# Attention's opening, four mask transfers a head, and an order planned with other costs

## The chip, the core and the metric

The kernel runs on one core of a Trainium2 chip. The metric is the time of one execution in microseconds on the device. An execution before the change took 792.61 us (median of three, 789.0 to 793.27). Engines are named as in the profile: PE is TensorE, PEld its weight load, DVE VectorE, ACT ScalarE, POOL GpSimd, SP SyncE, whose queue issues nearly all transfers. A q behind a name (SPq) is the engine's own sequencer.

## The reference

Attention over 16 heads (2 batches of 8), 768 positions and 64 dimensions, in which a query sees only the keys of its own bucket, and then two MoE-like layers on the result:

```python
q_bits = (np.einsum('bhsd,dk->bhsk', q, proj) > 0)      # 6 bits; k_bits likewise
mask = q_bucket[:, :, :, None] == k_bucket[:, :, None, :]
scores = np.where(mask, scale * q @ k.T, -1e9)
attn = np.exp(scores - max); attn = attn / (np.sum(attn) + 1e-09)
out = attn @ v                                         # x: 1536 tokens x 512
x = (h * tanh(softplus(h))) @ w_out,  h = x @ w_in     # first layer, w_in 512x2048
x = elu(h) @ w_out,  h = x @ w_in                      # second layer
```

## The kernel before, in words

All is float32. A product in full precision is made of three products of a high and a low part (`fp32r`); so nearly every operand exists twice, as a cast (high) and a subtraction (low).

**A head.** `prepare(g)` reads the head's k and q (`rw`, 64 rows each), splits them into `z` (high L343, low L345) and moves the halves by four transfers inside SBUF (L350 to L354) into the operand `qkt`, a tile of four slots. The bits of the buckets come from nine small matmuls (`project`, tile `pj`) of z against the random projection `sp`; a threshold (L368) turns the sums into masks (`bits`: 1 or -2^60), and six transfers (`mask`, L373) carry them into rows 64 to 75 of two slots of `qkt`. `V` is read and split for two heads at a time (L381 to L388).

**A tile** is 128 queries against 768 keys (`tile_ops`, six a head, 96 in all, numbered 0 to 95). Its scores `st` are eight matmuls: four over slots of 128 rows (the products of high and low parts) and four over 76 rows (the other products and the mask rows, which add 0 for equal buckets and a huge negative number otherwise). VectorE takes the row maximum (`pt`, `mx`, `nb`), ScalarE the exponential with the sum (`sm`). Two tiles at a time then go through `value_ops`: transposes on TensorE (`tu`), high part by ScalarE (`pth`), low part by VectorE (`ptl`), products with V (`xt`). ScalarE copies `xt` out (`xr`).

**A pair of heads.** When the second head of a pair is done, transfers on SP (`xs`, `xr`, L498 to L504) bring the halves together, GpSimd adds them (L506), TensorE transposes the reciprocals of the sums (`r`, L484), VectorE multiplies (L513), and x is split into `x_hi` and `x_lo`. `xt`, `pj` and `r` share a ring of two PSUM buffers.

**What sets the order.** Operations are recorded with a cost for each engine that may do them, a latency, a priority and the buffers they use; `Plan.run` simulates the engines with these numbers and emits the instructions in the planned order, engine by engine. On the chip each engine then does its list strictly in this order, and waits where an operand or buffer isn't ready. Priorities of the steps come from the tables `OFF` and `ODD`, in units of a tile; `CH` says which engines may do a step. A transfer on SP costs 450 in the plan (ns), and lands after a latency of 2300 to 6000. The MoE phase (`moe`) is planned the same way after it.

Of the kernel before, what the change touches and what calls it, by code (L numbers as in the profile page):

```python
# [10 lines left out]
F32R = mybir.dt.float32r  # L11
# [24 lines left out]
WARM = 10  # L36
NEARLY = 3
# [4 lines left out]
OFF = {'rh': -12.0, 'cp': -4.75, 'ld': -12.75, 'sp': -2.0, 'pj': 1.5, 'bits': -14.75, 'mk': -5.5, 'v': -13.5, 'S': 0.0, 'max': -0.25, 'exp': 12.0, 'sum': -5.25, 'T': 0.25, 'hi': 7.5, 'lo': -5.25, 'R': 7.0, 'pv': 2.0, 'xc': -6.25, 'xa': -34.25, 'xn': 3.25, 'xh': -6.5, 'xm': 9.25}  # L42
ODD = {'lo': [-0.5, 2.0, -1.5, -1.0, -4.5, 0.0], 'T': [-4.5, 1.0, 0.5, 0.0, 0.0, 1.0], 'pv': [3.0, 1.5, 0.0, -0.5, -0.5, -0.5], 'exp': [2.5, 1.5, 0.5, 1.0, 2.0, 0.0], 'hi': [1.0, -2.0, -2.5, 0.0, 3.0, 1.0], 'S': [1.0, 0.0, 1.0, 0.0, 0.5, 0.0], 'xc': [1.0, 0.0, 0.0, 1.0, 2.0, 0.0], 'max': [1.0, 0.5, 0.5, 0.5, 3.0, 2.0]}
# [142 lines left out]
def kernel(ctx, tc, qk, v, w, tab, out):  # L186
# [13 lines left out]
    NB = 6  # L200
# [85 lines left out]
    def attention(p, ap, pss, pst, psx, h_r):  # L286
        ident = ap.tile([128, 128], F32, name="ident")
        cst = ap.tile([128, 2 + NR], F32, name="cst")
        sp = ap.tile([128, 2, 384], F32R, name="sp")
        least, value = cst[:, 0:1], cst[:, 1:2]  # L290

        def tables(e):


            nc.vector.tensor_scalar(out=cst[:, 2 + NB:2 + 3 * NB], in0=cst[:, 2 + NB:2 + 3 * NB], scalar1=-1.0, scalar2=None,
                                    op0=ALU.mult)
            pr = cst[:, 2:2 + NR].unsqueeze(1).to_broadcast([128, 3, NR])
            hi, lo = (sp[:, j].rearrange("p (c n) -> p c n", c=3)[:, :, 0:NR] for j in range(2))
            nc.vector.tensor_copy(out=hi, in_=pr)
            nc.vector.tensor_tensor(out=lo, in0=pr, in1=f32(hi), op=ALU.subtract)  # L300
# [9 lines left out]
        bits_r = ring(2, [128, TH], F32R, "bits")  # L310
# [22 lines left out]
        def prepare(g):  # L333

            pr = NQ * g

            def at(name):
                return pr + OFF[name] if g else -50

            wt, rw, z = Buf(w_r, f"qkt{g}"), Buf(rw_r, f"rw{g}"), Buf(z_r, f"z{g}")  # L340
            ld = p.op({SP: 450}, lambda e: nc.sync.dma_start(out=rw.tile, in_=qk[g]), (), [rw], at('ld'), lat=4000)
# [24 lines left out]
            o = p.op({PE: 1080}, project, [lo, first[0]], [z, pj], at('pj'))  # L366
            bits = Buf(bits_r, f"bits{g}")
            o = p.op({DVE: dve(TH) + 110}, lambda e: nc.vector.tensor_scalar(  # L368
                out=bits.tile, in0=pj.tile[:, 0:TH], scalar1=least, scalar2=value, op0=ALU.is_ge, op1=ALU.mult),
                [o], [pj, bits], at('bits'))  # L370

            def mask(r, slot, c):
                return lambda e: nc.sync.dma_start(out=f32(wt.tile[64:64 + 2 * NB, slot, c * TH:(c + 1) * TH]),  # L373
                                                   in_=f32(bits.tile[32 * c + r:32 * c + r + 2 * NB]))
# [3 lines left out]
            kv[g] = wt, deps  # L378
            if g % 2 == 0:
                vr, vt = Buf(vr_r, f"vr{g}"), Buf(vt_r, f"vt{g}")  # L380
                ld = p.op({SP: 450}, lambda e: nc.sync.dma_start(out=vr.tile, in_=v[g // 2]), [deps[3]], [vr], pr - 4, lat=6000)  # L381

                def v4():
                    return vr.tile.rearrange("p k (j d) -> p k j d", j=2)
                h = p.op(pick('v', {ACT: act(S, False), DVE: 500, POOL: 1100}),
                         lambda e: copy(e, vt.tile[:, :, :, 0:64], v4()), [ld], [vr, vt], pr + OFF['v'])
                lo = p.op({POOL: pool(S)}, lambda e: sub(
                    e, vt.tile[:, :, :, 64:128], v4(), f32(vt.tile[:, :, :, 0:64])), [h], [vr, vt], pr + OFF['v'])  # L388
                V[g // 2] = (vr, vt, ld, lo)

        def tile_ops(i):

            g, t = steps[i]
            wt, wdeps = kv[g]
# [22 lines left out]
            o = p.op({ACT: act(S, False) + 140}, lambda e: nc.scalar.activation(  # L417
# [5 lines left out]
            if t == NQ - 1 or late and t % 2:  # L423
                r = slice(t - 1 if late else 0, t + 1)
                s = p.op(pick('eps', {DVE: 70, POOL: 250}), lambda e: eng(e).tensor_scalar(
                    out=sm.tile[:, r], in0=sm.tile[:, r], scalar1=1e-9, scalar2=None, op0=ALU.add),
                    sums[r], [sm], order(i, 'sum'))
                s = p.op({DVE: 76}, lambda e: nc.vector.reciprocal(out=rc.tile[:, r], in_=sm.tile[:, r]),
                         [s], [sm, rc], order(i, 'sum'))
                n = r.stop - r.start  # L430
                s = p.op({POOL: 150 + 80 * n}, lambda e: nc.gpsimd.tensor_copy(
                    out=rb.tile[:, r, g % 2], in_=rc.tile[:, r].unsqueeze(2).to_broadcast([128, n, 64])),
                    [s], [rc, rb], order(i, 'sum'))
                for j in range(r.start, r.stop):
                    ready.setdefault(j, []).append(s)
# [7 lines left out]
        def value_ops(i):  # L443
# [44 lines left out]
            if g < BH - 2:  # L488
# [26 lines left out]
                h = p.op(pick('xh', {ACT: act(S, False), DVE: 500, POOL: 1100}), lambda e: copy(e, x_hi[:, kt, to], xe.tile),  # L515
# [22 lines left out]
        def setup():  # L538
            nc.vector.memset(f32(sp), 0.0)
            make_identity(nc, ident)  # L540
            first[0] = p.op({ACT: 700}, lambda e: nc.scalar.dma_start(out=cst, in_=tab), (), (), -1e4, 2700)
            p.op({ACT: 1300}, lambda e: nc.scalar.preload_act_table_set("exp_and_others"), [first[0]], (), -1e3)
# [13 lines left out]
        first = [None]  # L556
# [215 lines left out]
```

## Time and profile before

| | |
|---|---|
| runs | 789.0, 792.61, 793.27 us |
| the profiled execution | 792.94 us, span from first to last instruction 791.2 us |
| mean granted clock of TensorE | 0.986 of full |
| PE busy | 763.6 us (97%) |
| DVE, ACT, POOL busy | 594.5, 418.3, 290.5 us |

Attention fills the span up to about 260 us, the MoE layers the rest. The shares of the whole span mix the two, so the rows below are taken by stretch. "Granted clock" is the share of full speed that the chip allowed TensorE.

### The profile page before, as it was taken

The numbers are of one execution on the slowest core, as the hardware profiler recorded it, in microseconds if no ns is written. First come the engines' busy times: TensorE is split into PE (matmuls) and PEld (weight loads), VectorE is DVE, ScalarE is ACT, GpSimd is POOL, SyncE is SP. The second block draws the span as 40 slices with busy tenths as digits, with TensorE's granted clock in tenths as the row PEclk, the third lists the DMA queues.
The fourth block names the chain that finished last, engine by engine and source line by source line (L and its number), as shares of the span: only waits on it lengthen the run. The fifth ranks groups of instructions, "written<-read, shape, count | busy, mean of one in ns | idle before, by whom it ended". The sixth has DMA issues, their size and how long they took to land.

```text
span 791.2 us, 11274 instructions
## 1 busy us (share of the span) xinstructions
PE 763.6 (97%) x4042; PEld 662.8 (84%) x4042; DVE 594.5 (75%) x1084; ACT 418.3 (53%) x800; POOL 290.5 (37%) x248
## 2 busy tenths in 40 slices
PE   4999999999988999999999999999999999999998
PEld 3998998998987888888888888888888888888886
DVE  2787798888779875456756776699977789989852
ACT  0686787877777654443433333447555434444420
POOL 3345355345133242323223332783323342233320
PEclk8899999999999999999999999999999999999999
DMA  6485555555431132111221122111221112121112
GB/s 173 135 217 138 151 154 147 143 142 132 115 97 51 54 107 80 54 54 55 80 80 54 53 66 78 44 54 55 88 97 55 53 54 81 54 80 54 54 66 94
DMA packets 24728, 71.07 MB, mean 90 GB/s; under 512 B 4256, under 2 KB 5408, under 8 KB 24672
## 3 DMA queue, kind: packets, MB, share of 16 engines
q1 hardware_dynamic: 24528, 70.34, 29.8%
q8 instruction: 32, 0.52, 0.3%
q14 instruction: 24, 0.20, 0.1%
q10 hardware_dynamic: 144, 0.01, 0.0%
HBM read 43.00 MB, written 3.15 MB: 58 GB/s over the span
## 4 chain that ended last, share of the span: by engine, by line
PE 83%; DVE 6%; DMA 4%; ACT 3%; SPq 2%; POOL 1%; issue 1%; DVEq 0%; ACTq 0%; POOLq 0%
PE h L580 66%; PE xt L472 5%; PE st L409 5%; PE tu L459 5%; DVE ptl L235 3%; DVE pt L412 2%; PE pj L363 2%; ACT pt L417 2%; DMA xr<-xr 2%; DMA wraw<-in_w_dram 1%; SPq L373 1%; ACT pth L464 1%; POOL xr L506 1%; SPq L349 1%; DVE xr L513 0%
## 5 line engine op out<-in xcount | busy, mean ns | idle before, releaser
L235 POOL TENSOR_TENSOR wt<-wt,whi 128x512 f32<-128x512 f32 x64 | 84.0, 1313 | 318.0 <-ACT whi L230 312.6
L580 PE MATMUL h<-x_hi,whi 128*128 128x512 f32 x384 | 149.7, 390 | 0.0
L580 PE MATMUL h<-glo,whi 128*128 128x512 f32 x384 | 149.4, 389 | 0.0
L580 PE MATMUL h<-x_hi,wlo 128*128 128x512 f32 x384 | 149.4, 389 | 0.0
L580 PE MATMUL h<-x_lo,whi 128*128 128x512 f32 x384 | 149.4, 389 | 0.0
L580 PE MATMUL h<-ghi,whi 128*128 128x512 f32 x384 | 149.4, 389 | 0.0
L580 PE MATMUL h<-ghi,wlo 128*128 128x512 f32 x384 | 149.4, 389 | 0.0
L417 ACT ACTIVATE pt<-pt,nb 128x768 f32<-128x768 f32 x96 | 90.2, 940 | 43.8 <-DVE nb L415 42.7
L235 DVE TENSOR_TENSOR ptl<-tu,pth 128x512 fp32r<-128x512 f32 x144 | 96.3, 687 | 16.8 <-ACT pth L464 16.4
L264 ACT ACTIVATE ws<-wraw 128x512 f32<-128x512 f32 x64 | 43.4, 678 | 117.0 <-POOL wlo L282 112.4
L409 PE MATMUL st<-qkt 76*128 76x384 f32 (+1 forms) x384 | 88.2, 359 | 10.8 <-DMA qkt<-bits 6.3
L412 DVE TENSOR_SCALAR_CACHE_REDUCE pt<-st 128x768 f32<-128x768 f32 x96 | 90.0, 949 | 9.0 <-PE st L409 8.9
L464 ACT CAST pth<-tu 128x512 fp32r<-128x512 f32 x144 | 82.4, 586 | 21.9 <-PE tu L459 20.1
L282 POOL TENSOR_TENSOR wlo<-wt,ws 128x512 fp32r<-128x512 f32 x64 | 86.1, 1346 | 6.7 <-DVE ws L277 2.0
L235 DVE TENSOR_TENSOR glo<-h,ghi 128x512 fp32r<-128x512 f32 x96 | 65.4, 687 | 28.8 <-ACT ghi L230 28.4
L459 PE MATMUL tu<-ident,pt 128*128 128x128 f32 x576 | 84.5, 278 | 2.2 <-DVE ptl L235 1.5
L580 PEld LDWEIGHTS h<-ghi,whi 128*128 128x128 f32 x384 | 72.1, 188 | 15.1
L580 PEld LDWEIGHTS h<-glo,whi 128*128 128x128 f32 x384 | 72.1, 188 | 15.0 <-DVE glo L235 0.2
L580 PEld LDWEIGHTS h<-x_hi,wlo 128*128 128x128 f32 x384 | 72.1, 188 | 15.0
L580 PEld LDWEIGHTS h<-ghi,wlo 128*128 128x128 f32 x384 | 72.1, 188 | 14.9
L680 DVE TENSOR_TENSOR y_acc<-h,y_acc 128x512 f32<-128x512 f32 x72 | 48.3, 687 | 48.2 <-PE h L580 48.1
L580 PEld LDWEIGHTS h<-x_hi,whi 128*128 128x128 f32 x384 | 72.1, 188 | 14.8
(64 smaller groups left out, 1250.3 us busy)
## 6 DMA issues: line engine op xcount, KB each, us to landing
wraw<-in_w_dram SPq DMA_DIRECT2D x64, 512.0 KB
qkt<-z SPq DMA_DIRECT2D x32, 384.0 KB
rw<-in_qk_dram SPq DMA_DIRECT2D x16, 384.0 KB
qkt<-z SPq DMA_DIRECT2D x32, 192.0 KB
vr<-in_v_dram SPq DMA_DIRECT2D x8, 384.0 KB
out_dram<-y_acc SPq DMA_DIRECT2D x12, 256.0 KB
xs<-xr SPq DMA_DIRECT2D x14, 192.0 KB
qkt<-bits SPq DMA_DIRECT2D x96, 12.0 KB
```

What stands on the lines that cost most here:

```text
L235: eng(e).tensor_tensor(out=out, in0=a, in1=b, op=ALU.subtract)
L264: o1 = p.op({ACT: act(n, False)}, lambda e: nc.scalar.activation(out=s.tile, in_=high().bitcast(F32), func=AF.Square), [ld], [raw, s], prio)
L282: o9 = p.op({POOL: pool(n)}, lambda e: nc.gpsimd.tensor_tensor(out=flat(lo), in0=t.tile, in1=s.tile, op=ALU.add), [o6, o8], [t, s, lo], prio)
L363: nc.tensor.matmul(pj.tile[:, 0:TH], lhsT=sp[:, b, c * 96:c * 96 + 128], rhs=z.tile[:, a, c * TH:(c + 1) * TH], start=(n == 0), stop=(n == 8))
L409: nc.tensor.matmul(st.tile[:, c, 0:HS], lhsT=wt.tile[0:n, q, t * 128:(t + 1) * 128], rhs=wt.tile[0:n, 2 + q, c * HS:(c + 1) * HS], start=( ...
L412: o = max_op = p.op({DVE: dve(S)}, lambda e: nc.vector.tensor_scalar(out=half(pt.tile), in0=st.tile[:, :, 0:HS], scalar1=-MASKED / SCALE, ...
L417: o = p.op({ACT: act(S, False) + 140}, lambda e: nc.scalar.activation(out=pt.tile, in_=pt.tile, func=AF.Exp, bias=nb.tile, scale=SCALE, ac ...
L459: nc.tensor.transpose(tu.tile[:, k, j], pt.tile[:, (2 * b + k) * 128:(2 * b + k + 1) * 128], ident)
L464: o = p.op({ACT: act(512)}, lambda e, tu=tu, ks=ks: nc.scalar.copy(out=hi.tile[:, ks], in_=flat(tu)), [o], [tu, hi], order(i, 'hi'))
L472: nc.tensor.matmul(xt.tile[:, 0:TH], lhsT=vt.tile[:, k, g % 2], rhs=m.tile[:, k], start=(k == 0 and j == 0), stop=(k == NKT - 1 and j == 1))
L580: nc.tensor.matmul(t.tile, lhsT=a.tile[:, k], rhs=r, start=(k == 0 and j == 0), stop=(k == 3 and j == 2))
L680: y = p.op({DVE: dve(n)}, lambda e, ya=ya, t=t: nc.vector.tensor_tensor(out=ya, in0=t.tile, in1=ya, op=ALU.add), [x, Y[m, c]], [t], prio)
```

## The change

- Head 0's masks are no longer transferred: four VectorE instructions (`direct`) write them into the operand, 12 rows x 384 columns each. Two of head 0's four operand copies may be issued from ScalarE's queue.
- For the other heads the projection works on two halves of 384 columns (six matmuls for nine), the threshold is 384 wide, and four mask transfers take the place of six.
- The tables for the projection are made before z is split, not after.
- Head 1's z is cast by ScalarE. The addition of 1e-9 moves from GpSimd to VectorE (`CH['eps']`).
- After head 1's projection, TensorE multiplies zeros 16 times (`hold`).
- The planner's numbers change: SP costs 400 to 760 for 450, latencies of 2200 to 4600 for 2300 to 4300, a dearer exponential, cheaper GpSimd casts; `OFF` and `ODD` are replaced.

```diff
-OFF = {'rh': -12.0, 'cp': -4.75, 'ld': -12.75, ...
+OFF = {'rh': 27.75, 'cp': -6.25, 'ld': 29.75, ...
-CH = {'rh': ('POOL',), 'v': ('POOL',), 'xh': ('ACT', 'POOL'), 'eps': ('POOL',)}
+CH = {'rh': ('POOL',), 'v': ('POOL',), 'xh': ('ACT', 'POOL'), 'eps': ('DVE',)}
...
-            h = p.op({DVE: 500} if g == 0 else pick('rh', {DVE: 500, ACT: act(S, False), POOL: 1100}),
+            h = p.op({DVE: 500} if g == 0 else {ACT: act(S, False)} if g == 1 else pick('rh', {..., POOL: 830}),
...
-                return lambda e: nc.sync.dma_start(out=f32(out()), in_=f32(in_()))
+                return lambda e: (nc.scalar if e == ACT else nc.sync).dma_start(out=f32(out()), in_=f32(in_()))
+            two = {SP: 650, ACT: 400} if g == 0 else {SP: 650}
-            if g == 0:
-                first[0] = p.op({DVE: 450}, tables, [first[0], lo], (), -50)
...
                 for a, b in ((0, 0), (0, 1), (1, 0)):
-                    for c in range(3):
-                        nc.tensor.matmul(pj.tile[:, 0:TH], lhsT=sp[:, b, c * 96:c * 96 + 128],
-                                         rhs=z.tile[:, a, c * TH:(c + 1) * TH], start=(n == 0), stop=(n == 8))
+                    for c in range(2):
+                        nc.tensor.matmul(pj.tile[:, 0:HS], lhsT=sp[:, b, 64 * (1 - c):64 * (1 - c) + 128],
+                                         rhs=z.tile[:, a, c * HS:(c + 1) * HS], start=(n == 0), stop=(n == 5))
...
-            for c in range(3):
-                for r, slot in ((0, 1), (2 * NB, 3)):
-                    deps.append(p.op({SP: 450}, mask(r, slot, c), [o], [bits, wt], at('mk'), lat=2300))
+            if g == 0:
+                def direct(e, c, s):
+                    r = slice(64 * c + 32 * s, 64 * c + 32 * s + 2 * NB)
+                    nc.vector.tensor_scalar(out=wt.tile[64:64 + 2 * NB, 1 + 2 * s, c * HS:(c + 1) * HS], in0=pj.tile[r, 0:HS],
+                                            scalar1=cst[r, 0:1], scalar2=cst[r, 1:2], op0=ALU.is_ge, op1=ALU.mult)
+                for c, k in ((0, 1), (1, 1), (0, 0), (1, 0)):
+                    deps.append(p.op({DVE: dve(HS)}, lambda e, c=c, k=k: direct(e, c, k), [o], [pj, wt], at('bits')))
+            else:
...
+                for c in range(2):
+                    for k in range(2):
+                        deps.append(p.op({SP: 760}, mask(c, k), [o], [bits, wt], at('mk'), lat=2700))
...
-                    XS[g // 2] = xs, p.op({SP: 450}, ..., parts, [xr, xs], order(i, 'xm'), lat=2300)
+                    XS[g // 2] = xs, p.op({SP: 650}, ..., parts, [xr, xs], order(i, 'xm'), lat=3000)
...
+            if i == 0:
+                hold = Buf(tu_r, "hold")
+                p.op({PE: 175 * HOLD}, lambda e: spin(HOLD, hold), [kv[1][2]], [hold], -40)
```

What it does to the order, at three places. First SP's list from the start, before (`rw` is a head's read, `qkt<-z` the operand copies, `qkt<-bits` the masks, `vr` V; the number is the head):

```order
L341 DMA rw1_103<-in_qk_dram 128x768
L349 DMA qkt0_111<-z0_106 64x2x768
L349 DMA qkt0_111<-z0_106 64x768
L349 DMA qkt0_111<-z0_106 64x1536
L349 DMA qkt0_111<-z0_106 64x768
L341 DMA rw2_130<-in_qk_dram 128x768
L349 DMA qkt1_132<-z1_108 64x2x768
L349 DMA qkt1_132<-z1_108 64x768
L349 DMA qkt1_132<-z1_108 64x1536
L373 DMA qkt0_111<-bits0_135 12x256 x6
L381 DMA vr0_158<-in_v_dram 128x768
L373 DMA qkt1_132<-bits1_150 12x256 x6
```

and after:

```order
L342 DMA rw1_103<-in_qk_dram 128x768
L350 DMA qkt0_114<-z0_109 64x2x768
L350 DMA qkt1_118<-z1_111 64x2x768
L350 DMA qkt0_114<-z0_109 64x768
L350 DMA qkt1_118<-z1_111 64x768
L350 DMA qkt1_118<-z1_111 64x1536
L350 DMA qkt1_118<-z1_111 64x768
L342 DMA rw2_160<-in_qk_dram 128x768
L342 DMA rw3_164<-in_qk_dram 128x768
L382 DMA qkt1_118<-bits1_162 12x384 x3
L390 DMA vr0_174<-in_v_dram 128x768
L382 DMA qkt1_118<-bits1_162 12x384
```

Head 0's masks and two of its copies (now in ScalarE's list) are gone from SP; V stands behind one more read and three masks of head 1.

TensorE's list from the start, before (`st` with the tile's number, `pj` with the head's):

```order
L553 MATMUL warm_89<-x_lo_65 128x384 x10
L363 MATMUL pj0_120<-z0_106,sp_82 128x256 x9
L363 MATMUL pj1_137<-z1_108,sp_82 128x256 x9
L409 MATMUL st0_166<-qkt0_111 128x384 x4
L409 MATMUL st1_172<-qkt0_111 128x384 x4
L363 MATMUL pj2_183<-z2_156,sp_82 128x256 x9
L409 MATMUL st2_198<-qkt0_111 128x384 x4
```

and after:

```order
L563 MATMUL warm_89<-x_lo_65 128x384 x10
L363 MATMUL pj0_120<-z0_109,sp_82 128x384 x6
L363 MATMUL pj1_131<-z1_111,sp_82 128x384 x6
L563 MATMUL hold_143<-x_lo_65 128x384 x16
L418 MATMUL st0_169<-qkt0_114 128x384 x4
L418 MATMUL st1_176<-qkt0_114 128x384 x4
L418 MATMUL st2_190<-qkt0_114 128x384 x4
```

The zero products stand between the second projection and the first scores, and the third projection has gone behind eight score tiles.

SP's list where heads 4 and 5 are done and head 8 is prepared, before:

```order
L349 DMA qkt8_1551<-z8_1197 64x1536
L349 DMA qkt8_1551<-z8_1197 64x768
L373 DMA qkt8_1551<-bits8_1571 12x256 x6
L502 DMA xs4_1408<-xr5_1489 64x768
L504 DMA xr4_1254<-xr5_1489 64x768
L381 DMA vr8_1654<-in_v_dram 128x768
```

and after:

```order
L350 DMA qkt8_1550<-z8_1240 64x1536
L350 DMA qkt8_1550<-z8_1240 64x768
L511 DMA xs4_1379<-xr5_1426 64x768
L513 DMA xr4_1193<-xr5_1426 64x768
L390 DMA vr8_1667<-in_v_dram 128x768
L382 DMA qkt8_1550<-bits8_1686 12x384 x4
```

The two transfers of x have moved from behind the masks to ahead of them, and V too.

## Rows read from the trace of the kernel before

**Rows 1.** Windows, attention proper and MoE: stretch, length, busy us, clock, DMA.

```profile
30.00:236.00 206.00, 195.76 (x1464) 190.03 (x1463) 170.72 (x417) 160.48 (x341) 85.89 (x83) 0.98 0.56 144
260.00:787.00 527.00, 527.00 (x2348) 436.70 (x2346) 388.10 (x590) 233.36 (x412) 185.35 (x139) 1.00 0.19 67
```

**Rows 2.** Timeline of PE, five of the projections: start, length, in brackets idle before.

```profile
38.58 1.24 PE L363 MATMUL pj<-z,sp 128*128 128x256 f32 x9
...
143.97 1.23 PE L363 MATMUL pj<-z,sp 128*128 128x256 f32 x9
...
159.89 1.34 PE L363 MATMUL pj<-z,sp 128*128 128x256 f32 x9 [1.42 <-DVE xr L513]
...
173.68 1.24 PE L363 MATMUL pj<-z,sp 128*128 128x256 f32 x9
...
235.35 1.23 PE L363 MATMUL pj<-z,sp 128*128 128x256 f32 x9
```

**Rows 3.** Groups by line, 30 to 236 us: busy us, mean ns, idle before.

```profile
L417 ACT ACTIVATE pt<-pt,nb 128x768 f32<-128x768 f32 x85 | 79.9, 940 | 19.2 <-DVE nb L415 18.1
L412 DVE TENSOR_SCALAR_CACHE_REDUCE pt<-st 128x768 f32<-128x768 f32 x83 | 77.6, 949 | 0.0
...
L368 DVE TENSOR_SCALAR bits<-pj,cst 128x256 fp32r<-128x256 f32 x12 | 6.5, 539 | 0.7 <-PE pj L363 0.2
L513 DVE TENSOR_TENSOR xr<-r,xr 128x384 f32<-128x384 f32 x12 | 6.3, 552 | 14.0 <-POOL xr L506 13.4 <-PE r L484 0.6
L484 PE MATMUL r<-ident,rb 128*128 128x128 f32 x36 | 6.2, 284 | 0.0
...
L428 DVE RECIPROCAL rc<-sm 128x6 f32<-128x6 f32 (+1 forms) x15 | 2.7, 180 | 1.6 <-POOL sm L425 1.6
```

**Rows 4.** The chain that ended last, 143 to 163 us: start, us, what.

```profile
143.43 0.71 PE st L409 x4
...
148.64 0.26 ACT xr L230
...
153.81 3.44 DMA xr<-xr
...
157.42 1.84 POOL xr L506
```

**Rows 5.** Timeline of SP's queue, at the opening and at that boundary.

```profile
13.14 5.58 SPq L373 DMA_DIRECT2D qkt<-bits  x6
...
147.51 5.64 SPq L373 DMA_DIRECT2D qkt<-bits  x6
153.25 0.52 SPq L502 DMA_DIRECT2D xs<-xr  x1
```

**Rows 6.** Timeline of PE, 0 to 31 us.

```profile
8.55 3.57 PE L363 MATMUL pj<-z,sp 128*128 128x256 f32 x15 [1.12 <-DVE sp L300]
12.33 0.59 PE L409 MATMUL st<-qkt 128*128 128x384 f32 x2 [0.22 <-DMA qkt<-z]
18.49 0.66 PE L409 MATMUL st<-qkt 76*128 76x384 f32 x1 [5.57 <-DMA qkt<-bits]
...
29.90 0.36 PE L472 MATMUL xt<-pth,vt 128*128 128x256 f32 x1
```

**Rows 7.** Windows in the opening, columns as in rows 1 (PE, PEld, DVE, ACT, POOL).

```profile
5.00:15.00 10.00, 5.05 (x21) 3.99 (x20) 4.51 (x6) 0.00 (x0) 4.37 (x4) 0.83 0.91 226
12.00:15.00 3.00, 0.71 (x3) 0.30 (x2) 0.55 (x1) 0.00 (x0) 1.26 (x2) 1.00 1.09 292
20.00:25.00 5.00, 5.00 (x19) 5.00 (x20) 2.60 (x7) 1.54 (x3) 2.66 (x2) 0.50 0.28 89
```

**Rows 8.** Timeline of DVE, 0 to 12 us.

```profile
4.84 0.96 DVE L235 TENSOR_TENSOR z<-rw,z 128x768 fp32r<-128x768 f32 x1
```

**Rows 9.** Timeline of POOL, 0 to 35 us.

```profile
21.88 0.82 POOL L232 CAST vt<-vr 128x768 fp32r<-128x768 f32 x1 [5.51 <-DMA vr<-in_v_dram]
22.78 1.84 POOL L235 TENSOR_TENSOR vt<-vr,vt 128x768 fp32r<-128x768 f32 x1
```

More of the change, by code (lines that the diff above doesn't have):

```diff
@@ L36 @@
 WARM = 10
+HOLD = 16
 NEARLY = 3
@@ L296, in tables @@
                                     op0=ALU.mult)
-            pr = cst[:, 2:2 + NR].unsqueeze(1).to_broadcast([128, 3, NR])
-            hi, lo = (sp[:, j].rearrange("p (c n) -> p c n", c=3)[:, :, 0:NR] for j in range(2))
+            pr = cst[:, 2:2 + NR].rearrange("p (s n) -> p s n", s=2)
+            hi, lo = (sp[:, j, 64:128].rearrange("p (s n) -> p s n", s=2)[:, :, 0:2 * NB] for j in range(2))
             nc.vector.tensor_copy(out=hi, in_=pr)
@@ L340, in prepare @@
             wt, rw, z = Buf(w_r, f"qkt{g}"), Buf(rw_r, f"rw{g}"), Buf(z_r, f"z{g}")
-            ld = p.op({SP: 450}, lambda e: nc.sync.dma_start(out=rw.tile, in_=qk[g]), (), [rw], at('ld'), lat=4000)
-            h = p.op({DVE: 500} if g == 0 else pick('rh', {DVE: 500, ACT: act(S, False), POOL: 1100}),
+            ld = p.op({SP: 400}, lambda e: nc.sync.dma_start(out=rw.tile, in_=qk[g]), (), [rw], at('ld'), lat=4000)
+            h = p.op({DVE: 500} if g == 0 else {ACT: act(S, False)} if g == 1 else pick('rh', {DVE: 500, ACT: act(S, False), POOL: 830}),
                      lambda e: copy(e, z.tile[:, 0], rw.tile), [ld], [rw, z], at('rh'))
@@ L365, in project @@
                         n += 1
[L366 to L374, printed above, removed]
@@ L375, in prepare, with mask @@
-            for c in range(3):
-                for r, slot in ((0, 1), (2 * NB, 3)):
-                    deps.append(p.op({SP: 450}, mask(r, slot, c), [o], [bits, wt], at('mk'), lat=2300))
-            kv[g] = wt, deps
+            o = pj_op = p.op({PE: 1050}, project, [lo, first[0]], [z, pj], at('pj'))
+            if g == 0:
[6 more added lines that the diff above has]
+            else:
+                bits = Buf(bits_r, f"bits{g}")
+                o = p.op({DVE: dve(HS)}, lambda e: nc.vector.tensor_scalar(
+                    out=bits.tile, in0=pj.tile[:, 0:HS], scalar1=least, scalar2=value, op0=ALU.is_ge, op1=ALU.mult),
+                    [o], [pj, bits], at('bits'))
+                def mask(c, s):
+                    r = slice(64 * c + 32 * s, 64 * c + 32 * s + 2 * NB)
+                    return lambda e: nc.sync.dma_start(out=f32(wt.tile[64:64 + 2 * NB, 1 + 2 * s, c * HS:(c + 1) * HS]),
+                                                       in_=f32(bits.tile[r]))
+                for c in range(2):
+                    for k in range(2):
+                        deps.append(p.op({SP: 760}, mask(c, k), [o], [bits, wt], at('mk'), lat=2700))
@@ L540, in setup @@
             make_identity(nc, ident)
-            first[0] = p.op({ACT: 700}, lambda e: nc.scalar.dma_start(out=cst, in_=tab), (), (), -1e4, 2700)
-            p.op({ACT: 1300}, lambda e: nc.scalar.preload_act_table_set("exp_and_others"), [first[0]], (), -1e3)
+            ld = p.op({ACT: 700}, lambda e: nc.scalar.dma_start(out=cst, in_=tab), (), (), -1e4, 2200)
+            p.op({ACT: 1300}, lambda e: nc.scalar.preload_act_table_set("exp_and_others"), [ld], (), -1e3)
+            first.append(p.op({DVE: 450}, tables, [ld], (), -1e3))
             warm = Buf(tu_r, "warm")
@@ L554, in spin @@
                                  start=True, stop=True)
-        first = [None]
+        first = []
         last, gates = [], []
@@ L744 @@
         tab[(D if r < 2 else 0):(2 * D if r < 2 else D), 2 + r * NB:2 + (r + 1) * NB] = proj
-    for c in range(3):
-        tab[32 * c:32 * c + NB, 0] = tab[32 * c + 3 * NB:32 * c + 4 * NB, 0] = TINY
-        tab[32 * c:32 * c + 2 * NB, 1] = 1.0
-        tab[32 * c + 2 * NB:32 * c + 4 * NB, 1] = -BIG
+    for c in (0, 64):
+        tab[c:c + NB, 0] = tab[c + 32 + NB:c + 32 + 2 * NB, 0] = TINY
+        tab[c:c + 2 * NB, 1] = 1.0
+        tab[c + 32:c + 32 + 2 * NB, 1] = -BIG
     units = []
```

43 lines of the change are left out of this document (22 added, 21 removed).

## The prediction

> **What bounds the kernel now.** I read the busy time by stretch first [rows 1]. From 260 us to 787 us, in the two MoE layers, TensorE is busy for 527.00 of 527.00 us at full clock. Nothing in that code changes, so I take this stretch as it is: whatever the change does, it moves the moment at which attention hands over. In attention proper (30 to 236 us) TensorE is busy 195.76 of 206 us, VectorE 170.72 and ScalarE 160.48. TensorE is the nearest to a bound, but the waits have to be read one by one.
>
> To see what they cost TensorE I go by the projection, which comes once a head [rows 2]; its bracket at 159.89 says that it waited for the normalisation of x (L513). From its run at 159.89 to that at 173.68 are 13.79 us: a head without a wait. The head before took 159.89 - 143.97 = 15.92 us. From 38.58 to 235.35 thirteen heads pass, 196.77 us, against 13 x 13.79 = 179.3 us: 17.5 us too many. At most 6.2 us of it is honest work, the transposes of the reciprocals (L484, [rows 3]). So 11.3 us are lost at pair boundaries, with the slow clock that follows some waits.
>
> The cause of one such loss is in the chain [rows 4]. x of the odd head is copied out by 148.90 (148.64 + 0.26), but the transfer of it starts only at 153.81, lands 3.44 us later, GpSimd adds until 159.26, VectorE multiplies, and only then the projection has a buffer. In the DMA queue one sees why the transfer was late [rows 5]: SP issues six mask transfers from 147.51 to 153.15, 0.94 us apiece, and the two transfers of x stand behind them, the first at 153.25. VectorE, which takes its work in order, sits through 13.4 us of such waits over the stretch [rows 3].
>
> The opening is a story of its own [rows 6]. The first score matmuls run at 12.33, when head 0's operands have landed, and the next at 18.49, after 5.57 us of waiting: the second part of the contraction is the mask rows, and they come by six small transfers that SP issues from 13.14 on [rows 5]. The first product with V comes at 29.90. TensorE's granted clock is 0.50, its lower level (1.2 GHz), while it is busy from 20 to 25 us [rows 7].
>
> **The change, part by part.** *Head 0's masks.* Six transfers go; VectorE writes them straight into the operand in four instructions of 12x384. The nearest rows are the 256-wide threshold (L368) at 539 ns and the 384-wide multiply (L513) at 552 ns [rows 3], so 4 x 0.55 = 2.2 us. The projection's tables are now made before the split of z instead of after it, and with them gone from the path projection 0 can start when z's low half is done, at about 5.8 (4.84 + 0.96, [rows 8]). At the lower clock, as the 15 matmuls that took 3.57 us [rows 6] (256 columns each, 0.24 us), its 2304 columns take about 2.2 us, so the masks are in place by some 10.2.
>
> *Head 0's operands.* Two of the four copies are issued from ScalarE's queue, and head 1's are interleaved. In the row of 5 to 15 us the DMA engines were 0.91 busy and moved 226 GB/s [rows 7]. Head 0's 1.15 MB with up to 0.5 MB of head 1's ahead of it need 7 us from 4.84: about 12, where they landed before. A second issuing queue gives nothing as long as bytes are the limit. The Trainium skill has a rule that speaks against this part of the change (DMA: Bandwidth & Descriptors, section Issuing engines are not separate DMA queues): several issuers share the same engines and only save the time to issue. By it the operands land near 12; were a second queue worth more bandwidth, they would land near 10, and the sum would be the same by either, since the next item ends later.
>
> *The zero products.* Sixteen matmuls of 384 columns stand between projection 1 and the first score. Their price per matmul lies between 0.18 us (four score matmuls of that width in 0.71 us, [rows 4]) and 0.36 us (the fifteen projection matmuls of 256 columns in 3.57 us, [rows 6], are 0.24 each, times 384/256): 2.8 to 5.7 us. Projection 1 needs the split of head 1's z, now a cast on ScalarE and a subtraction on GpSimd: some 2.7 us, as V's in [rows 9], from about 5.2 on (its read is the next behind head 0's, which had landed and been cast by 4.84). So it starts near 8 and ends near 10, so the first score starts at 12.9 to 15.7. What it waited for is then there. I take 13.3: after the warm start, nearly continuous work from 5.8 on looks like that from 8.55 to 12.12 [rows 6], after which the granted clock is 1.00 [rows 7].
>
> *What is late next: V.* Six score tiles follow in a row, two buffers deep, at the pace at which VectorE takes their maxima (0.95 us, L412, [rows 3]): from 13.3 they are done before 20. V's transfer now stands behind two more reads and three masks. The bytes ahead of it are 2 x 1.15 + 2 x 0.39 MB, at 226 GB/s 13.6 us: V lands at about 20, GpSimd works through z2, z3 (2 x 2.7 us; z2's read is in by 17) and then V (0.82 + 1.84, [rows 9]) and the first product with V comes at 25.6, against 29.90: 4.3 us sooner. TensorE has by then done one more score tile, one more projection and four more transposes than at 29.90 before, about 2.2 us. Opening: **-6.5 us**. Bounds: -3.3 (products with V 1 us later still, since the zero products all ran at the lower clock, and nothing of the extra work of use) and -9.4 (bytes no limit: z2 in by 14.7, three splits of 2.7 us on GpSimd, products from 22.7, all extra work of use).
>
> *Four mask transfers for six, and their place.* In the order shown for SP at head 8 the two transfers of x now stand right behind the operand copies, and the masks last. At the boundary of [rows 4] that starts them 4.4 us sooner (153.25 against 148.90), more than the 2.1 us that this head took above 13.79; all of that wait goes. Masks get later by the three transfers now ahead of them, some 0.6 us each, but four of them at 0.94 cost 1.9 us less than six: about even. Behind the masks on SP stand the next head's read and copies, and who waits for a late mask is the first score tile of the next head and all of TensorE's list behind it; that is in the bound below.
>
> *The recomputed order.* It moves nearly everything else too. Its costs now include 0.65 to 0.76 us an issue where it had 0.45, near the 0.52 to 0.94 of [rows 5]. I expect most of the 11.3 us back, not all, since ScalarE and VectorE are busy for 78 and 83% of that stretch: **-8 us**, bounds 0 (all of it comes back as other waits) and -11.3.
>
> *Onto VectorE.* The 1e-9 goes from GpSimd to VectorE, 20 instructions; nearest row the reciprocal (L428), 180 ns [rows 3], so 3.6 us at most. 15 masks are 384 wide instead of 256: by the 552 ns row 0.01 us more each, if time went with columns 0.27 each, 4.0 us. VectorE has 35 us idle from 30 to 236 us [rows 1], so I count **+1** (bounds 0 and +7.6). In its favour: the 1.6 us for which the reciprocal waited for GpSimd [rows 3] can't come back.
>
> **Sum.** The profiled execution took 792.94 us (span 791.2), 0.33 above the median of 792.61. 792.9 - 6.5 - 8 + 1 = 779.4, which I give as **779.5 us**.
>
> **Rivals.** (A) *Only the opening comes.* The three engines are so close that waits removed at the boundaries turn up elsewhere, above all as VectorE waiting for ScalarE's casts (the 78 and 83% above). 792.9 - 6.5 + 1 = 787.4. Against it: heads without a boundary run at 13.79 us with the same work. Chance 0.19. (B) *V or the clock eats the opening, and the order gives nothing:* 792.9 - 3.3 + 1 = 790.6, within the bound of no change. Chance 0.10. (C) *Slower: the sum's wait moves onto VectorE.* The 1e-9 instruction can only run when the head's last exponential is done. On GpSimd that wait was free; on VectorE everything behind it waits, maxima and low halves first. In the new order only about one more maximum and one low half of VectorE's work stand between the last tile's maximum and it, and the exponential takes 0.94 (L417, [rows 3]). If ScalarE is late by 1 us at each of 20 places, that is 20 us: 792.9 - 6.5 - 8 + 20 = 798.4. It decides from 0.73 us a place on. Against it: that tile's exponential stands early enough in ScalarE's list to fit beside those two. Chance 0.06. The forecast has 0.62, and 0.03 is left for faster than its bounds.
>
> **Numbers.** The likeliest is 779.5, its own range 772 (792.9 - 9.4 - 11.3) to 785 (792.9 - 3.3 - 5.6 + 1, half of the 11.3). The range reaches up through rival A, to 788.5, and down to 771. About 0.5% (4 us) is what a measurement of this kernel can tell from no change. Faster: forecast, A and the tail below, 0.84; same 0.10 (B); slower 0.06 (C).
>
> **What would show it.** Right: a full first set of scores near 13 to 14 with no mask transfer before it; first product with V at 24 to 27; the transfers of x issued before the masks of the next head; no wait of VectorE for GpSimd's addition of x above 1 us; 14.0 to 14.5 us a head; hand-over to the MoE near 246 instead of 260; 527 us after it as before. Wrong: heads of 15 us with waits for casts or for masks, or a first product with V as late as 29.

## The result, and the profile after

The changed kernel takes 781.56 us (median of four, 781.22 to 784.36), beside 791.99 for the kernel before in the same comparison: a ratio of 0.9881 [0.9845, 0.9918]. Forecast were 779.5 us, range 771.0 to 788.5. The profiled execution took 781.22 us, its span 779.4 (before 792.94 and 791.2).

Windows of the kernel after: the opening, attention proper, and MoE; columns as in [rows 1].

```profile
5.00:15.00 10.00, 6.13 (x30) 5.24 (x30) 4.50 (x7) 0.83 (x1) 1.93 (x1) 1.00 0.89 196
20.00:25.00 5.00, 5.00 (x25) 4.76 (x24) 4.20 (x12) 3.74 (x7) 4.32 (x4) 0.71 0.30 95
30.00:236.00 206.00, 198.76 (x1476) 193.09 (x1475) 182.95 (x449) 162.48 (x349) 85.59 (x71) 0.99 0.55 143
245.00:772.00 527.00, 525.88 (x2347) 435.16 (x2346) 391.50 (x598) 236.30 (x419) 187.23 (x140) 1.00 0.19 66
```

In MoE TensorE is busy for 525.88 of 527 us, before for all of them. So nothing is gained there; in attention TensorE is busy 3 us more of the same 206 us.

The opening, timeline of TensorE after, against [rows 6]:

```profile
5.22 2.31 PE L363 MATMUL pj<-z,sp 128*128 128x384 f32 x10
...
8.36 2.94 PE L563 MATMUL hold<-x_lo 128*128 128x384 f32 x16
14.79 1.81 PE L418 MATMUL st<-qkt 128*128 128x384 f32 x8 [3.50 <-DMA qkt<-z]
16.79 5.63 PE L418 MATMUL st<-qkt 128*128 128x384 f32 x16 [0.19 <-DVE pt L421]
...
27.89 0.38 PE L481 MATMUL xt<-pth,vt 128*128 128x256 f32 x1
```

No mask transfer is waited for any more. The zero products end at 11.3 and TensorE then idles 3.50 us until head 0's operands land. SP's queue, VectorE and GpSimd in the same stretch say why, and what became of masks and V:

```profile
5.19 7.45 SPq L350 DMA_DIRECT2D qkt<-z  x6
12.69 1.65 SPq L342 DMA_DIRECT2D rw<-in_qk_dram  x2
...
16.91 0.51 SPq L390 DMA_DIRECT2D vr<-in_v_dram  x1
```
```profile
6.87 2.77 DVE L370 TENSOR_SCALAR qkt<-pj,cst 12x384 fp32r<-12x384 f32 x4 [0.71 <-PE pj L363]
```
```profile
19.20 0.82 POOL L233 CAST z<-rw 128x768 fp32r<-128x768 f32 x1 [11.35 <-DMA rw<-in_qk_dram]
...
26.00 1.84 POOL L236 TENSOR_TENSOR vt<-vr,vt 128x768 fp32r<-128x768 f32 x1
```

Six copies of heads 0 and 1 take SP 7.45 us to issue, 1.24 each; the masks are in place by 9.64; V is split by 27.84, and the first product with V runs at 27.89, against 29.90 in [rows 6].

At the boundaries, the waits (engine, line, for whom: total us, times, longest). Of TensorE before, beside VectorE's 13.4 us of [rows 3]:

```profile
PE pj L363 <- DVE xr L513: 4.6, 3, 1.7
PE st L409 <- DVE pt L412: 4.1, 2, 3.0
```

Of VectorE and TensorE after:

```profile
DVE xr L522 <- POOL xr L515: 9.5, 5, 3.5
...
PE st L418 <- DVE pt L421: 6.2, 8, 2.8
```

In all TensorE waits 10.2 us from 30 to 236 us before, and 7.1 after, of which 5.7 are in the last row (its 6.2 are of the whole span). The waits are fewer, not gone. The longest of them, where heads 10 and 11 are done: SP's queue, GpSimd, VectorE and TensorE after.

```profile
195.22 3.24 SPq L350 DMA_DIRECT2D qkt<-z  x4
198.58 1.80 SPq L511 DMA_DIRECT2D xs<-xr  x1
200.42 0.60 SPq L513 DMA_DIRECT2D xr<-xr  x1
201.07 0.69 SPq L390 DMA_DIRECT2D vr<-in_v_dram  x1
202.50 3.12 SPq L382 DMA_DIRECT2D qkt<-bits  x4
```
```profile
206.43 1.80 POOL L515 TENSOR_TENSOR xr<-xr,xs 128x768 f32<-128x768 f32 x1 [4.18 <-ACT xr L231]
```
```profile
208.26 0.56 DVE L522 TENSOR_TENSOR xr<-r,xr 128x384 f32<-128x384 f32 x1 [3.45 <-POOL xr L515]
```
```profile
209.84 0.94 PE L418 MATMUL st<-qkt 128*128 128x384 f32 x4 [2.80 <-DVE pt L421]
```

x's transfers do stand ahead of the masks, but behind four operand copies, and GpSimd adds x 6 us after the second one was issued. (The bracket of that addition names a copy by ScalarE that ended just then; this x was copied out by 197.52, and the trace has the last part of its second transfer landing at 206.27.) VectorE sits in front of the multiplication of x (L522), the next row maximum behind it comes late, and TensorE waits for that.

To see where each kernel gains, this table takes the timelines of ScalarE: the start of the copy of `xt` to `xr` that ends each odd head, and from one to the next (two heads; 27.6 without a wait, by the 13.79 us of the prediction, though some pairs come out up to 0.5 us below that).

| kernel | end of head 1 | heads 2, 3 | 4, 5 | 6, 7 | 8, 9 | 10, 11 | 12, 13 |
|---|---|---|---|---|---|---|---|
| before | 57.04 | 31.52 | 30.04 | 29.94 | 29.71 | 29.88 | 31.78 |
| after | 52.29 | 27.12 | 30.95 | 29.79 | 27.27 | 29.75 | 32.35 |
| e7, before with x first | 56.43 | 28.01 | 29.71 | 29.58 | 28.01 | 28.04 | 27.81 |
| e6, after with x last | 52.69 | 31.56 | 37.23 | 36.96 | 28.91 | 35.89 | 36.96 |
| e9, 1e-9 on GpSimd | 52.94 | 27.12 | 30.49 | 29.99 | 27.89 | 31.28 | 33.43 |
| e11, old tables | 52.34 | 28.82 | 30.70 | 31.89 | 28.85 | 29.77 | 29.89 |
| e13, old order, x first | 58.84 | 32.64 | 31.15 | 29.51 | 28.08 | 28.06 | 27.76 |
| e14, x before the copies | 52.55 | 32.82 | 32.56 | 29.33 | 33.91 | 27.66 | 27.79 |

After against before: 4.75 us up to the end of head 1, 5.64 over the next six pairs (4.40 and 2.44 of it at two of them; the other four give 0.15 us at most, and two of these lose), and 1.4 behind that, of 11.8 in all between the two profiled executions. By the medians it is 10.4.

### The profile page after: what moved, and what is told of

Read it like the earlier page. It is cut to its first block, busy times and chain, and to the rows that moved or that the text cites. A ratio compares the mean times of both kernels' runs of the same rounds, so it can differ in the third digit from the quotient of the medians.

```text
span 779.4 us, 11177 instructions
## 1 busy us (share of the span) xinstructions
PE 761.2 (98%) x4010; PEld 660.3 (85%) x4010; DVE 602.6 (77%) x1107; ACT 416.6 (53%) x800; POOL 287.0 (37%) x228
## 4 chain that ended last, share of the span: by engine, by line
PE 85%; DVE 6%; DMA 4%; ACT 3%; POOL 2%; issue 1%; SPq 0%; POOLq 0%; ACTq 0%; DVEq 0%
PE h L593 67%; PE st L418 6%; PE xt L481 6%; PE tu L468 5%; DVE pt L421 2%; DVE ptl L236 2%; ACT pt L426 1%; PE pj L363 1%; POOL xr L515 1%; DMA xr<-xr 1%; DMA qkt<-z 1%; ACT pth L473 1%; DMA xs<-xr 1%; DVE xr L522 1%; DMA cst<-in_tab_dram 0%
## 5 line engine op out<-in xcount | busy, mean ns | idle before, releaser
L418 PE MATMUL st<-qkt 76*128 76x384 f32 (+1 forms) x384 | 86.3, 355 | 9.7 <-DVE pt L421 6.2
L473 ACT CAST pth<-tu 128x512 fp32r<-128x512 f32 x144 | 80.2, 586 | 18.2 <-PE tu L468 17.9
L593 PEld LDWEIGHTS h<-x_lo,whi 128*128 128x128 f32 x384 | 72.1, 188 | 14.7
```

Of the source, the lines that this page charges most:

```text
L418: nc.tensor.matmul(st.tile[:, c, 0:HS], lhsT=wt.tile[0:n, q, t * 128:(t + 1) * 128], rhs=wt.tile[0:n, 2 + q, c * HS:(c + 1) * HS], start=( ...
L473: o = p.op({ACT: act(512)}, lambda e, tu=tu, ks=ks: nc.scalar.copy(out=hi.tile[:, ks], in_=flat(tu)), [o], [tu, hi], order(i, 'hi'))
L593: nc.tensor.matmul(t.tile, lhsT=a.tile[:, k], rhs=r, start=(k == 0 and j == 0), stop=(k == 3 and j == 2))
```

## The experiments

Theory A of these runs (not rival A of the prediction) is what the forecast rests on: the gain has two sources that are apart, the opening and the place of x's transfers on SP. The first four runs undo or do one part alone. Where an edit moves instructions in a list, the other engines' lists stay as they were.

**e7: the kernel before, with nothing but x's transfers moved** ahead of the six masks of the next even head.

```diff
+    for g in range(1, 13, 2):
+        ahead(lists["SP"], f"x{g}", f"mk{g + 3}")
```

> The kernel before, with one change: on SP the two transfers of x at a pair's end stand ahead of the six mask transfers of the next even head (heads 4 to 14), every other list as it was. Theory A (the boundaries were lost to mask issues ahead of x on SP): VectorE's wait for the addition of x falls from 13.4 us to under 4, and the kernel is 6 to 9 us faster, 783 to 786. Rival B (the gain at the boundaries comes from the recomputed order as a whole): less than 2 us, 790 to 792.

Measured 780.72 us (780.12 to 781.0), ratio 0.9868 [0.9852, 0.9885]. SP's queue at the boundary of [rows 5], and the wait of VectorE:

```profile
144.12 0.46 SPq L564 DMA_DIRECT2D xs<-xr  x1
144.68 0.55 SPq L567 DMA_DIRECT2D xr<-xr  x1
145.28 4.63 SPq L433 DMA_DIRECT2D qkt<-bits  x6
```
```profile
DVE xr L577 <- POOL xr L570: 2.4, 4, 1.1
```

The order of one queue, at six places, is worth as much as the whole change, and some 2 us more than this run's forecast. VectorE's 13.4 us of waiting become 2.4, TensorE's 10.2 become 3.5, and the six pairs take 171.16 us, 11.7 less than before; from head 8 on a pair takes 28 us.

**e6: the changed kernel with x's transfers behind the four masks.** The same edit the other way round (`behind` for `ahead`).

> The changed kernel, with one change: on SP the two transfers of x at a pair's end stand behind the four mask transfers of the next even head, as before; every other list as it is. Theory A: the waits for x come back, 4 issues of 0.8 us each time, 5 to 10 us slower than the changed kernel, 786 to 791. Rival B: at most 2 us slower, 781 to 784.

Measured 812.42 us (809.68 to 812.95), ratio 1.0262 [1.0233, 1.0291].

```profile
DVE xr L586 <- POOL xr L579: 32.1, 6, 7.1
```
```profile
PE st L480 <- DVE pt L483: 18.4, 5, 6.2
```

The sign is the expected one and the size is not: 31 us. VectorE and SP's queue where heads 4 and 5 are done (up to 130 us):

```profile
127.45 0.67 DVE L436 TENSOR_SCALAR bits<-pj,cst 128x384 fp32r<-128x384 f32 x1
```
```profile
128.15 2.36 SPq L442 DMA_DIRECT2D qkt<-bits  x3
```

This x was copied out by 121.84, and its first transfer goes out at 131.38. In the new order the masks come later beside x than before: their threshold runs on VectorE only at 127.45, and SP begins with them 6 us after x is ready, where in [rows 4] and [rows 5] it began 1.4 us ahead of that. So whoever stands behind them waits longer. Four masks alone would not have saved this order.

**e2: the changed kernel, head 0's masks by four transfers** from a threshold tile, instead of the direct writes.

```diff
-                    deps.append(p.op({DVE: dve(HS)}, lambda e, c=c, k=k: direct(e, c, k), ...
+                    deps.append(p.op({DVE: dve(HS)}, lambda e, c=c, k=k: carry(c, k), ...
```

> The changed kernel with head 0's masks again by a threshold and four transfers on SP, every compute list as it is. Theory A (the masks were the first wait of the opening and their going is worth some 4 us): first full set of scores at 18 instead of 16, 2 to 4 us slower, 783.5 to 785.5. Rival C (V sets the end of the opening): first product with V within 0.5 us of 27.9 and the time unchanged, 781 to 782.

Measured 784.92 us (784.22 to 785.77), ratio 0.9923 [0.9905, 0.994]. TensorE's opening in this run:

```profile
15.10 0.98 PE L426 MATMUL st<-qkt 128*128 128x384 f32 x2 [3.49 <-DMA qkt<-z]
18.63 7.00 PE L426 MATMUL st<-qkt 76*128 76x384 f32 x22 [2.55 <-DMA qkt<-bits]
```

The wait for masks is back. It is 2.55 us instead of 5.57 [rows 6] not because four masks are in place sooner (TensorE goes on at 18.63, before at 18.49), but because the operands come later (15.10 against 12.33). The first product with V comes at 30.75, 2 us after V is split, so it is not V that sets it. The median is 3.4 us above the changed kernel's, as forecast, although the two intervals just overlap. The direct write is the only part of the opening whose going shows in the time.

**e8: x's transfers issued from ScalarE's queue** (`nc.scalar` for `nc.sync` in both), past everything on SP.

> The changed kernel with the 14 transfers of x at the pairs' ends issued from ScalarE's queue instead of SP's (where they stand behind 1.15 MB of operand copies). Theory D (what is left of the boundary waits, 9.5 us on VectorE, is x behind those copies in one queue): VectorE's wait under 4 us, 3 to 6 us faster than the changed kernel, 775.5 to 778.5. Rival E (both queues share the same engines, so x lands as late): within 1 us of 781.5.

Measured 782.91 us (781.2 to 783.4), ratio 0.9893 [0.9873, 0.9913]. The boundary after heads 10 and 11 again, issue and addition:

```profile
200.60 0.47 ACTq L511 DMA_DIRECT2D xs<-xr  x1
201.22 1.43 ACTq L513 DMA_DIRECT2D xr<-xr  x1
```
```profile
209.25 1.82 POOL L515 TENSOR_TENSOR xr<-xr,xs 128x768 f32<-128x768 f32 x1 [3.18 <-DMA xr<-xr]
```

From the end of the copy-out (200.57) to the addition it is 8.7 us, beside four copies that SP issues from 198.27 on; on SP's queue in the changed kernel it is 8.9. VectorE still waits 8.2 us for x, where Theory D had less than 4; no gain. The Trainium skill (DMA: Bandwidth & Descriptors, section Issuing engines are not separate DMA queues) says that transfers from several issuers run on the same engines and only the time to issue is saved; this run agrees (8.7 us against 8.9).

**e1, e3, e4, e5: the opening.** e1 leaves out the zero products. e3 issues head 0's copies ahead of head 1's on SP. e4 reads V early, on ScalarE's queue, and splits it ahead of z2. e5 does both.

```diff
-                p.op({PE: 175 * HOLD}, lambda e: spin(HOLD, hold), [kv[1][2]], [hold], -40)
+                p.op({PE: 175 * HOLD}, lambda e: None, [kv[1][2]], [hold], -40)
...
+    behind(lists["SP"], "cp1", "cp0")
...
+    ahead(lists["POOL"], "vsplit", "z2")
```

> The changed kernel without the 16 zero products, every other list as it is. Theory F (they end at 11.3, 3.5 us before head 0's operands land, and neither delay the scores nor hold the clock, which falls at 16.1 all the same): first scores still at 14.8, time within 1 us of the changed kernel, 781 to 782. Rival G (they keep the clock up for the opening): the clock is at its lower level from about 12 on, scores slower, 1 to 3 us more.

> The changed kernel with head 1's first operand copy behind head 0's on SP. Theory H (head 0's operands land late, at 14.7, because head 1's 0.38 MB are ahead of a part of them): first scores at 13.0 to 13.5, but V at 27.8 still sets the first product, so the time is within 1 us of the changed kernel. Rival I (the scores set the opening): 1 to 1.8 us faster, 780.

> The changed kernel with V of heads 0 and 1 read at the start from ScalarE's queue and split on GpSimd before heads 2 and 3. Theory H (V sets the first product): first product at 25 to 26 instead of 27.9 (limited then by the low halves and the projections ahead of it), 1 to 3 us faster, 778.5 to 780.5. Rival I: no faster, 781 to 782, or slower where the projections of heads 2 and 3 now wait for their split.

> Both of the two edits: head 0's operands first, and V early. Theory H: the gains add up once V is out of the way, first scores at 13.3, first product at 24 to 25, 2 to 4 us faster than the changed kernel, 777.5 to 779.5. Rival I: as head 0's operands alone.

Measured: e1 782.99 us, 0.9908 [0.9888, 0.9927]; e3 781.58, 0.9897 [0.9868, 0.9925]; e4 782.02, 0.9892 [0.9871, 0.9914]; e5 782.0, 0.989 [0.9873, 0.9907]. None differs measurably from the changed kernel. That is Theory H's forecast for e3 and rival I's for e4 and e5; e1, 1.4 us up by the medians, lies nearer to its rival G, within the noise. TensorE in e1, in e3 and in e5:

```profile
14.63 8.31 PE L418 MATMUL st<-qkt 128*128 128x384 f32 x24 [6.27 <-DMA qkt<-z]
...
28.50 0.28 PE L481 MATMUL xt<-pth,vt 128*128 128x256 f32 x1
```
```profile
12.71 1.64 PE L479 MATMUL st<-qkt 128*128 128x384 f32 x8 [1.30 <-DMA qkt<-z]
...
27.07 0.38 PE L542 MATMUL xt<-pth,vt 128*128 128x256 f32 x1 [1.78 <-POOL vt L295]
```
```profile
13.97 1.64 PE L491 MATMUL st<-qkt 128*128 128x384 f32 x8 [1.77 <-DMA qkt<-z]
...
27.35 0.28 PE L554 MATMUL xt<-pth,vt 128*128 128x256 f32 x1
```

Without the zero products TensorE waits for the operands all the longer, the granted clock from 14 to 24 us is 0.51, its lower level but for the end, in place of 0.66, and the first product with V comes 0.6 us later: the zero products earn little and cost nothing that shows. Head 0 first brings the scores to 12.71 at full clock; TensorE's list gets to the first product with V at 25.29, and then V is late by 1.78. With V early as well the operands land later again and the product comes at 27.35, 0.5 us sooner than in the changed kernel. TensorE waits for nothing there: the matmuls of its own list stand between, from 16 to 22 us at half clock. Up to the end of head 1 these four gain between -0.7 and +0.5 us; the 0.5 of e5 is gone by the end of head 13 (229.88, against 229.52 in the changed kernel).

**e9: the 1e-9 on GpSimd again**, nothing else moved.

```diff
-                s = p.op(pick('eps', {DVE: 70, POOL: 250}), lambda e: eng(e).tensor_scalar(
+                s = p.op(pick('eps', {DVE: 70, POOL: 250}), lambda e: nc.gpsimd.tensor_scalar(
```

> The changed kernel with the addition of 1e-9 on GpSimd again, nothing else moved. Forecast: within 1 us of the changed kernel (781 to 783): on VectorE it cost nothing that the trace shows. Rival C (VectorE waits there for the last exponential): faster by 3 us or more, below 779.

Measured 784.41 us (783.25 to 787.47), ratio 0.9923 [0.9899, 0.9946]: neither of the two. GpSimd and VectorE in this run, where heads 8 and 9 are done:

```profile
176.16 1.80 POOL L515 TENSOR_TENSOR xr<-xr,xs 128x768 f32<-128x768 f32 x1 [13.88 <-DMA xr<-xr]
178.04 0.23 POOL L434 TENSOR_SCALAR sm<-sm 128x6 f32<-128x6 f32 x1
```
```profile
178.31 0.19 DVE L437 RECIPROCAL rc<-sm 128x6 f32<-128x6 f32 x1 [4.61 <-POOL sm L434]
```

On GpSimd the 0.23 us instruction stands behind the addition of x, which waits for its transfer; the reciprocal, and with it VectorE, waits for x by this second way. VectorE waits 5.9 us for it in all. The move to VectorE, which the prediction counted as a cost, gains some 2.8 us by the medians; the two intervals just overlap, so this size is not certain.

**e11: the changed kernel with the old `OFF` and `ODD`.**

```diff
-OFF = {'rh': 27.75, 'cp': -6.25, 'ld': 29.75, ...
+OFF = {'rh': -12.0, 'cp': -4.75, 'ld': -12.75, ...
```

> The changed kernel with the old tables OFF and ODD, all else as changed (direct masks, four mask transfers, dearer SP issues). In the plan x's transfers again stand behind the masks of the next even head. Theory A (the gain at the boundaries comes from the place of x's transfers, which the tables set): the opening's 4 us stay, the boundaries go back to what they were: 786 to 789, VectorE's wait for GpSimd's addition of x above 10 us in all. Rival F (four masks in place of six and the new costs are enough): 780 to 783, that wait below 10 us.

Measured 785.32 us (784.09 to 788.04), ratio 0.9934 [0.9911, 0.9957], between the two forecasts. The premise of the expectation was wrong in part: with the new costs of SP's issues the planner puts x directly behind the copies at all six boundaries with the old tables too, and masks stand close ahead of it, with one copy between, at two of them only. VectorE waits 9.6 us for x, as in the changed kernel. The opening is the changed kernel's (52.34), and the six pairs take 179.92 us, against 182.87 before and 177.23 after. So by these profiled executions about half of the gain at the boundaries is in the tables, the other half in the planner's costs, the four masks and the 1e-9 on VectorE; the intervals of the two kernels just overlap, and the shares are rough.

**e13: the direct masks, four masks and zero products, with the old tables and costs, the 1e-9 on GpSimd, and x set ahead of the masks.** The two gains together, as Theory A has it.

```diff
-OFF = {'rh': 27.75, 'cp': -6.25, ...
+OFF = {'rh': -12.0, 'cp': -4.75, ...
-            two = {SP: 650, ACT: 400} if g == 0 else {SP: 650}
+            two = {SP: 450, ACT: 400} if g == 0 else {SP: 450}
...
+        ahead(lists["SP"], f"x{g}", f"mk{g + 3}")
```

> The changed kernel's edits (direct masks for head 0, four mask transfers, zero products), but the old tables and planner costs, the 1e-9 on GpSimd, and the two transfers of x set ahead of the masks of the next even head by a rule. Theory A (opening and boundaries are separate gains and add up): the opening's 4 us and the 10 to 12 us that the place of x's transfers gave in the kernel before, 776 to 779. Rival G (the opening's lead is waited away at the next boundaries, which have a pace of their own): 780 to 783, as much as either alone.

Measured 790.18 us (789.1 to 791.5), ratio 0.9985 [0.9968, 1.0002]: worse than either alone, and outside both forecasts. From head 8 on the pairs take 28.1, 28.1 and 27.8 us, as in e7; against e7, all is lost by head 5. The opening did come: the fifth of the six copies of heads 0 and 1 starts at 47.34, and at 51.47 in the kernel before. The sixth, at 58.84, is 1.8 us behind it. This first loss, on GpSimd, TensorE and VectorE:

```profile
49.73 0.83 POOL L293 CAST z<-rw 128x768 fp32r<-128x768 f32 x1 [6.16 <-DMA qkt<-z]
```
```profile
50.61 0.96 PE L423 MATMUL pj<-z,sp 128*128 128x384 f32 x4 [2.12 <-POOL z L293]
```
```profile
53.56 0.68 DVE L436 TENSOR_SCALAR bits<-pj,cst 128x384 fp32r<-128x384 f32 x1 [3.89 <-PE pj L423]
```

GpSimd gets a buffer for the next head's z only when the copies out of it have landed; TensorE's list has the projection of this z early, VectorE's the threshold, and both engines stop. That the order was planned with other costs, under which this z comes in time, is the likely reason; no run tests it. That x is ahead of the masks does not help an order that waits elsewhere.

**e14: the changed kernel, x's transfers ahead of the operand copies too.** What is left in the row of 198.58 above.

```diff
+    for g in range(1, 13, 2):
+        ahead(lists["SP"], f"x{g}", f"cp{g + 3}")
```

> The changed kernel with the two transfers of x of an odd head ahead of the four operand copies of the next even head too (heads 4 to 14), not only of its masks; no other engine's list differs. In the changed kernel x is copied out by 197.5 at one boundary, is issued behind the copies from 198.58 to 201.02, and is added only at 206.43, after which VectorE has waited 3.45 us and TensorE 2.8. Theory A carried on (what is left at the boundaries is x behind 1.15 MB of copies): x is added some 3 us sooner, VectorE's wait of 9.5 us and most of TensorE's 6.2 us for its maxima go, 776 to 779. Rival H (the copies now wait on SP until x is ready, 2 to 4 us, and head 4 to 14's operands or the reads behind them come late): 782 to 790, with new waits of TensorE for the copies or of GpSimd for a read.

Measured 789.59 us (787.25 to 790.6), ratio 0.9966 [0.9949, 0.9983]: the time of rival H. SP's queue, GpSimd, VectorE and TensorE at the first boundary:

```profile
52.95 0.53 SPq L577 DMA_DIRECT2D xs<-xr  x1
53.58 0.55 SPq L580 DMA_DIRECT2D xr<-xr  x1
54.22 3.39 SPq L412 DMA_DIRECT2D qkt<-z  x4
```
```profile
61.88 0.82 POOL L295 CAST z<-rw 128x768 fp32r<-128x768 f32 x1 [14.16 <-DMA qkt<-z]
...
64.88 1.80 POOL L583 TENSOR_TENSOR xr<-xr,xs 128x768 f32<-128x768 f32 x1
```
```profile
66.71 1.02 DVE L590 TENSOR_TENSOR xr<-r,xr 128x384 f32<-128x384 f32 x2 [4.70 <-POOL xr L583]
```
```profile
67.32 0.38 PE L547 MATMUL xt<-pth,vt 128*128 128x256 f32 x1 [3.69 <-DVE xr L590]
```

x is issued at once, but the copies behind it come 6 us later than in the changed kernel (54.22 against 48.37), and GpSimd's list has the cast of the next z, whose buffer they hold, ahead of the addition of x. So the addition comes at 64.88, against 59.50 in the changed kernel. The copies had slack for their readers on TensorE, and none for the buffer that they free; that is a third wait, beside the two that rival H names. It is not so everywhere: heads 10 to 13 take 27.66 and 27.79 us in this run, as short as in any.

## Why the prediction was right, and where it was not

The time and both directions came as forecast, 2 us above the sum. That the sum is so near is in part luck: the opening and the boundaries each gave less than forecast, 1.4 us came from behind head 13, where nothing was forecast, and four of the signs to look for just missed (first scores at 14.79, first product with V at 27.89, a wait of 3.5 us for x, 14.8 us a head). By its steps:

**Opening, -6.5: right in kind, too large.** Measured are -4.75 us to the end of head 1, inside the bounds of -3.3 and -9.4. Mis-sized was the landing of head 0's operands, "about 12": the first scores wait for them until 14.79. The step took bytes as the limit (the DMA engines are indeed 0.89 busy from 5 to 15 us), 1.65 MB of them from 4.84 on at 226 GB/s. The copies go out from 5.19, and up to the last landing at 14.66 the engines move 198 GB/s, which is 1.9 MB: more of head 1's copies goes along than the "up to 0.5 MB" of the step. e3, which only takes the first copy of head 1 out of the way, has the scores at 12.71. Behind the wait of 3.5 us the clock, which the step assumed at full level, is 0.66 from 14 to 24 us; in e3, with a wait of 1.3 us, it is 1.00, and in e5, with 1.77 us, 0.66 again. The direct masks took 0.69 us each where 0.55 were assumed, and cost nothing, since they were done 5 us ahead of need.

**V.** Forecast 25.6, measured 27.89. Two things end at about that time. V is split by 27.84, 2.2 us later than forecast: GpSimd takes z2 and z3 first, and z2's read lets it start only at 19.20, where the step had 17. And TensorE's own list, for some 6 us at half clock, is no sooner there: with V early the product still comes at 27.53 (e4) and 27.35 (e5). At full clock (e3) the list is there at 25.29 and waits for V. So V was rightly named, and what the step left out is the clock behind the wait for the operands. No run has both V early and the full clock.

**Boundaries, -8: the mechanism was right, the way to it only in part.** With the +1 for VectorE the prediction had -7; measured are -5.64 over the six pairs and -1.4 behind them. e7 shows the mechanism: in the old order x's place on SP alone removes the waits, and gives 11.7 us, all of the 11.3 that the prediction found lost there. e6 shows that the new order needs it too. The statement that "all of that wait goes" failed: VectorE still waits 9.5 us for x, longest 3.5, where the prediction allowed 1 us, while x now stands behind the copies. e8 and e14 show that neither another queue nor a place ahead of the copies brings this back. So part of the waits that the prediction feared to see come back did come back.

**The 1e-9, +1: most likely wrong in sign.** e9 makes it about -2.8 by the medians, with intervals that just overlap; the six pairs of e9 take 180.21 us, against 177.23. So some half of the 5.64 us may hang on a move that was counted as a cost. The prediction said of the reciprocal's wait only that 1.6 us [rows 3] "can't come back"; in the new order there would have been 5.9 us of it. Rival C did not occur: after the change no wait of VectorE for the exponential shows at that instruction.

**Pace.** Forecast 14.0 to 14.5 us a head; measured 177.23 / 12 = 14.8. Hand-over forecast at 246; the first MoE product is at 243.87, before at 259.25. These 15.4 us are more than was gained, for MoE's first products now stand among attention's last; the last copy of `xt` comes 10.3 us sooner (258.61, before 268.91).

**What stays open.** Why heads 12 and 13 take 32.35 us after, and 27.8 in e7, e13 and e14, was not taken apart: x's late addition is seen there, but other steps of the order differ too. Whether an order planned anew with x's place fixed would hold both gains was not tried. Nor was the gain at the boundaries split further among the tables, the costs, the four masks and the 1e-9. No version beat the changed kernel: e7's 780.72 us cannot be told from its 781.56.

## What to carry to other kernels

Read the queue of an engine that only issues, row by row, in front of each wait: what stands ahead of the urgent transfer, and does it have slack? A change of place in that list can be worth as much as a whole new plan (e7). But slack must be counted to the next user of every buffer that the delayed transfer frees, also on a third engine that does its list in order; and two gains measured apart need not add up (e13), since the order in between can wait elsewhere.

## What the runs showed of the hardware

The time of SP to issue a transfer depends on what is ahead of it: the first transfer of x took 1.80 us right behind four operand copies and 0.53 with nothing ahead, six copies 1.24 each on average in the opening and four copies 0.81 each later (3.24 us). A second issuing queue did not bring x in sooner (8.7 us from copy-out to addition in e8, 8.9 on SP). A transfer lands in parts, and the last decides: of the 16 landings that the trace has for x's second transfer at the boundary of heads 10 and 11, fifteen are in by 204.59 and the last at 206.27. The direct write of 12 rows took 0.69 us for 384 columns, and the threshold of 128 rows for as many columns 0.68 (e13): here the other 116 rows cost nothing.
